# Fewer weight groups converted ahead of the second stage, the rest beside its first units, and three token blocks visited twice

## The chip, the core and the metric

One core of a Trainium2 chip runs the whole program. The metric is the device time of one execution in microseconds (us). The engines are PE (matrix products, with PEld for its weight loads), DVE (VectorE), ACT (ScalarE), POOL (GpSimd) and SP, whose queue issues every DMA of this kernel. Each engine works through its own list of instructions in order.

## What is computed

Causal attention with a decay for 8 batches of 8 heads (576 rows, 64 columns a head), and then a feed-forward network on the 4608 rows of 512 columns that it leaves:

```
scores = q @ k.T / sqrt(64) + cum[:, None] - cum[None, :]   # cum: running sum of log(clip(f, 1e-4, 1))
attn = softmax(causal(scores)) ; x = attn @ v               # x: 4608 x 512
h = x @ w_in                                                # 512 x 2048
g = h * erf(softplus(h))
out = g @ w_out                                             # 2048 x 512
```

All values are float32.

## The kernel before

The program has two stages on the same engines.

**Attention.** A loop over `t` runs 64 half-steps and 5 more to drain. A half-step is half of the query blocks of a pair of heads. It is a software pipeline: at `t` the kernel forms the scores of half-step `t` (PE, `scores`), reduces them with the decay (DVE, `reduce`, L459), takes exponentials of `t-1` (ACT), scales those of `t-2` (`normalize`: a small sum and reciprocal on DVE, L476 and L477, the scaling `pr` on POOL, L481), transposes those of `t-3` (PE, L493; 12 transposes in an even half-step and 13 in an odd one), multiplies `t-4` with the values (PE, L520), and stores `t-5` (`xo`, L529 to L533, to `xt_d` in memory, L535). The order of the instructions of PE, ACT, DVE and POOL is that of the source; SP's is set by the scheduler.

**Weight conversion.** Into the same loop the kernel puts the conversion of the weights. They come as 64-bit words and are turned into float32 by integer operations on DVE and then split into a rounded high part and a low part, so that a product is three fast ones. The weights fall into `NU` = 8 groups, each of four pieces (two of `w_out`, two of `w_in`). For a piece, `words` issues three DVE operations (L333 to L335) and `joined` two (L342, L351). Both pieces of `w_in` end in one tile `wa`, of which there is a single buffer. POOL then forms sums of its blocks (`combine`, L370), ACT rounds (`out_high` L357, `in_high` L374), POOL subtracts the rounded part (`out_low` L362, `in_low` L380), and SP stores high and low parts to `wo_d` and `wi_d` (L358, L363, L375, L382). A table `work` holds these in steps, a group starting every 8 steps; one step is done per half-step from t = 4, and two from t = 60.

**Second stage** (class `Moe`). Tokens are taken in `NV` = 6 blocks of 768, features in the 8 groups; a unit is one group for one block, 48 units in all. x is split for one level of Strassen's scheme: three differences of halves, a fourth later (`sub`, L119), and each of seven terms is rounded (ACT, L125) and its rest taken (POOL, L129). `up(u)` has seven products of six matmuls (L165) into four PSUM banks `pha`, `phb`, `phx`, `phy`; the first four products open the banks, and the last three accumulate into `pha`, `phx` and `phy`, after DVE has copied or added what stood there (L171, L175). `activate` has softplus and erf on ACT, `gate` multiplies on DVE (L204, tile `e`), `round_gate` splits the result into `gh` (ACT) and `gl` (POOL, L212). `down(u, tb)` has six matmuls for each of six token tiles (L223), with four PSUM buffers `y`; `flush` adds `y` to `ys` in SBUF (DVE, L232, L235), and after the eighth group stores it. `middle(u)` issues `down(u)` on PE, and meanwhile the activation and gates of `u+1` between the flushes, then `prepare(u)` with some steps of the next block's x. Behind it stands `up(u+2)`. The first two `up` stand in the draining half-steps 64 to 67. Weights are loaded per unit, `wi` (L145) and `wo` (L151), each with two buffers.

Of the kernel before, what the change touches and what calls it, by code (L numbers as in the profile page):

```python
# [21 lines left out]
P = 128  # L22
# [38 lines left out]
X0 = 32  # L61
TABLES = "natural_log_exp_and_others"
# [9 lines left out]
class Moe:  # L72
# [39 lines left out]
    def x_steps(self, v):  # L112

        nc, raw = self.nc, self.raw

        def sub(name, a, b, kd):
            if kd == 0 and name not in ("12",):
                raw[v, name] = self.half(name, v)
            nc.gpsimd.tensor_tensor(out=raw[v, name][:, kd], in0=raw[v, a][:, kd], in1=raw[v, b][:, kd], op=ALU.subtract)  # L119

        def high(n, nm):
            pool = self.xq if v % 2 and n > 2 else self.xp
            self.xs[v, n] = x = pool.tile([P, 2, 2, TB], F32R, name=f"xs{v}_{n}", tag="xs",
                                          bufs=10 if pool is self.xp else 4)
            nc.scalar.copy(out=x[:, 0], in_=raw[v, nm])  # L125

        def low(n, nm, kd):
            x = self.xs[v, n]
            nc.gpsimd.tensor_tensor(out=x[:, 1, kd], in0=raw[v, nm][:, kd], in1=x[:, 0, kd].bitcast(F32),  # L129
                                    op=ALU.subtract)  # L130
# [11 lines left out]
    def load_wi(self, u):  # L142
        if u < self.n:
            self.wi[u] = w = self.wp.tile([P, 2, 7, 2, P], F32R, name=f"wi{u}", tag="wi", bufs=2)
            self.nc.sync.dma_start(out=w.rearrange("p h i k f -> p (h i k f)").bitcast(F32),  # L145
                                   in_=self.wi_d[u % NU])

    def load_wo(self, u):
        if u < self.n:
            self.wo[u] = w = self.wop.tile([P, 2, 2, DM], F32R, name=f"wo{u}", tag="wo", bufs=2)  # L150
            self.nc.sync.dma_start(out=w.rearrange("p f h e -> p (f h e)").bitcast(F32),  # L151
                                   in_=self.wo_d[u % NU])
# [73 lines left out]

    def flush(self, u, tb, y):
        nc = self.nc
        v, a = divmod(u, NU)
        if a == 0:  # L230
            self.y[v, tb] = self.yp.tile([P, DM], F32, name=f"ys{v}_{tb}", tag="ys", bufs=8)
            nc.vector.tensor_copy(out=self.y[v, tb], in_=y)  # L232
            return
        ys = self.y[v, tb]
        nc.vector.tensor_tensor(out=ys, in0=y, in1=ys, op=ALU.add)  # L235
        if a == NU - 1:
            row = v * NW + tb * P
            nc.sync.dma_start(out=self.out[row:row + P], in_=ys)

    def prepare(self, u):  # L240

        v, a = divmod(u, NU)
        if v + 1 == NV:
            return
        if a == 0:
            self.load_x(v + 1)
            self.later = self.x_steps(v + 1)
        else:
            for _ in range(-(-len(self.later) // (NU - 1 - a)) if a < NU - 1 else 0):
                self.later.pop(0)()  # L250

    def middle(self, u):
# [17 lines left out]


@with_exitstack
def attention_moe(ctx, tc, q2, k2, vp, f, w_in, w_out, out):
# [28 lines left out]

    moe = Moe(tc, xt_d, out, xp, wp)
    moe.wi_d, moe.wo_d = wi_d, wo_d

    moe_pools = ctx.enter_context(ExitStack())
    with ExitStack() as ph:
        early = ExitStack()
        cv = ph.enter_context(tc.tile_pool(name="cv", bufs=2))
# [17 lines left out]

        def words(u):

            raw = raws[u]  # L330
            tops[u] = top = cv.tile([P, DM], F32, name=f"wtop{u}", tag="wtop", bufs=3)
            topi = top.bitcast(I32)
            nc.vector.tensor_scalar(out=topi, in0=raw[1], scalar1=0x7FFFFFFF, scalar2=None, op0=ALU.bitwise_and)  # L333
            nc.vector.tensor_scalar(out=top, in0=top, scalar1=TINY, scalar2=None, op0=ALU.max)
            nc.vector.tensor_scalar(out=topi, in0=topi, scalar1=3, scalar2=0x3FFFFFFF,  # L335
                                    op0=ALU.logical_shift_left, op1=ALU.bitwise_and)

        def joined(u):

            a, i = divmod(u, 4)  # L340
            raw, topi = raws.pop(u), tops[u].bitcast(I32)
            nc.vector.scalar_tensor_tensor(out=topi, in0=raw[0], scalar=29, in1=topi,  # L342
                                           op0=ALU.logical_shift_right, op1=ALU.bitwise_or)
            out_, top, sign = topi, topi, raw[1]
            if i > 1:
                if i == 2:
                    sums[a] = cv.tile([P, 8, 2 * P], F32, name=f"wa{a}", tag="wa", bufs=1)
                out_ = (sums[a][:, 4:6] if i == 3 else sums[a][:, ::7]).bitcast(I32)
                top, sign = (x.rearrange("p (i n) -> p i n", i=2) for x in (top, sign))
                del tops[u]  # L350
            nc.vector.scalar_tensor_tensor(out=out_, in0=sign, scalar=-0x40000000, in1=top,  # L351
                                           op0=ALU.bitwise_and, op1=ALU.bitwise_or)
            load_weight(u + 2)

        def out_high(a, i):
            highs[a, i] = hi = cv.tile([P, DM], F32R, name=f"wohi{a}_{i}", tag="wohi", bufs=1)
            nc.scalar.copy(out=hi, in_=tops[4 * a + i])  # L357
            nc.sync.dma_start(out=wo_d[a][:, 2 * i * DM:(2 * i + 1) * DM], in_=hi.bitcast(F32))  # L358

        def out_low(a, i):  # L360
            top, hi = tops.pop(4 * a + i), highs.pop((a, i))
            nc.gpsimd.tensor_tensor(out=top, in0=top, in1=hi.bitcast(F32), op=ALU.subtract)  # L362
            nc.sync.dma_start(out=wo_d[a][:, (2 * i + 1) * DM:(2 * i + 2) * DM], in_=top)  # L363

        def combine(a, *which):
            w = sums[a]
            for n in which:
                x, y, op = {3: (7, 5, ALU.add), 2: (0, 7, ALU.subtract), 1: (3, 0, ALU.subtract),
                            6: (4, 1, ALU.subtract)}[n]
                nc.gpsimd.tensor_tensor(out=w[:, n], in0=w[:, x], in1=w[:, y], op=op)  # L370

        def in_high(a, lo, hi):
            highs[a] = part = cv.tile([P, 4, 2 * P], F32R, name=f"whi{a}_{lo}", tag="whi", bufs=1)[:, :hi - lo]
            nc.scalar.copy(out=part, in_=sums[a][:, lo:hi])  # L374
            nc.sync.dma_start(out=wi_d[a][:, lo * 256:hi * 256], in_=part.rearrange("p i f -> p (i f)").bitcast(F32))  # L375

        def in_low(a, *which):
            for lo, hi in which:
                w = sums[a][:, lo:hi]
                nc.gpsimd.tensor_tensor(out=w, in0=w, in1=highs[a][:, lo % 4:lo % 4 + hi - lo].bitcast(F32), op=ALU.subtract)  # L380
                if hi == 7:
                    nc.sync.dma_start(out=wi_d[a][:, 7 * 256:], in_=sums.pop(a)[:, :7].rearrange("p i f -> p (i f)"))  # L382

        work = defaultdict(list)
        for a in range(NU):
# [3 lines left out]
            for i in range(2):  # L389
                work[8 * a + 2 * i + 2].append((out_high, a, i))  # L390
                work[8 * a + 2 * i + 3].append((out_low, a, i))
# [270 lines left out]
```

## Time and profile before

| | |
|---|---|
| runs, us | 1203.05, 1198.08, 1201.11; median 1201.11 |
| profiled execution, us | 1199.8 |
| its span, first to last instruction, us | 1198.0 |
| mean granted TensorE clock | 0.966 |
| attention loop | to about 454 us |
| first down product | 461.98 us |
| chain that ended last | PE 61% of the span |

A row of a group of instructions gives line, engine, operation, output<-input, shapes and count, then busy time in us and the mean of one in ns, then the idle time of the engine before them and who ended it. A row of waits gives who waited for whom, the total in us, how often, and the longest. A row of the timeline gives start and length in us. A row of a stretch gives its length, the busy time of PE, PEld, DVE, ACT and POOL with their counts, the granted clock, the DMA share and GB/s. A row of one tile's instructions gives the shortest, median and longest in ns.

### The profile page before, as it was taken

The numbers are of one execution on the slowest core, as the hardware profiler recorded it, in microseconds if no ns is written. First come the engines' busy times: TensorE is split into PE (matmuls) and PEld (weight loads), VectorE is DVE, ScalarE is ACT, GpSimd is POOL, SyncE is SP. The second block draws the span as 40 slices with busy tenths as digits, with TensorE's granted clock in tenths as the row PEclk, the third lists the DMA queues.
The fourth block names the chain that finished last, engine by engine and source line by source line (L and its number), as shares of the span: only waits on it lengthen the run. The fifth ranks groups of instructions, "written<-read, shape, count | busy, mean of one in ns | idle before, by whom it ended". The sixth has DMA issues, their size and how long they took to land.

```text
span 1198.0 us, 21626 instructions
## 1 busy us (share of the span) xinstructions
PE 1102.8 (92%) x7552; PEld 973.9 (81%) x7552; DVE 801.6 (67%) x1899; ACT 697.0 (58%) x1519; POOL 606.6 (51%) x732
## 2 busy tenths in 40 slices
PE   5997979788697686999999999999999999999998
PEld 3886767667586575999999999999999999999997
DVE  4997979789797843666666555556666666665555
ACT  3785758576575552565555655555565556555553
POOL 2466657676676651555345534554455435552223
PEclk9998989898898898999999999999999999999999
DMA  6697997878778535556655675567555754566532
GB/s 246 205 318 251 330 314 281 277 258 256 248 254 292 190 132 207 194 193 234 230 188 191 246 247 181 180 221 244 186 194 216 266 200 176 184 214 221 193 132 88
DMA packets 66124, 265.94 MB, mean 222 GB/s; under 512 B 7008, under 2 KB 13152, under 8 KB 53728
## 3 DMA queue, kind: packets, MB, share of 16 engines
q1 hardware_dynamic: 66016, 264.56, 63.1%
q8 instruction: 60, 0.98, 0.3%
q14 instruction: 48, 0.39, 0.1%
HBM read 222.45 MB, written 42.09 MB: 221 GB/s over the span
## 4 chain that ended last, share of the span: by engine, by line
PE 61%; DMA 1%; DVE 0%; issue 0%; SPq 0%
PE y L223 33%; PE pha L165 8%; PE phy L165 8%; PE phx L165 8%; PE phb L165 4%; DMA wo<-wo_d 1%; DVE ys L235 0%; SPq L535 0%; SPq L151 0%
## 5 line engine op out<-in xcount | busy, mean ns | idle before, releaser
L212 POOL TENSOR_TENSOR gl<-e,gh 128x384 fp32r<-128x384 f32 x192 | 221.9, 1188 | 415.9 <-PE y L223 215.0
L223 PE MATMUL y<-wo,gh 128*128 128x512 f32 x1152 | 357.5, 391 | 8.8 <-DMA wo<-wo_d 8.8
L223 PEld LDWEIGHTS y<-wo,gh 128*128 128x128 f32 x1152 | 216.7, 189 | 52.4 <-issue 9.0
L481 POOL TENSOR_SCALAR pr<-pr,st 128x576 f32<-128x576 f32 (+4 forms) x320 | 164.4, 537 | 159.3 <-DVE st L477 120.7
L235 DVE TENSOR_TENSOR ys<-y,ys 128x512 f32<-128x512 f32 x252 | 174.3, 692 | 99.4 <-PE y L223 99.4
L223 PE MATMUL y<-wo,gl 128*128 128x512 f32 x576 | 225.8, 392 | 0.0
L471 ACT ACTIVATE pr<-pr,st 128x576 f32<-128x576 f32 (+3 forms) x320 | 176.7, 556 | 43.4 <-DVE st L459 43.2
L520 PE MATMUL o<-pt,v 128*64 128x128 f32 (+1 forms) x1920 | 116.8, 280 | 68.8 <-DVE xo L533 40.3
L520 PEld LDWEIGHTS o<-pt,v 128*64 128x64 f32 x1920 | 107.4, 151 | 79.7 <-DVE xo L533 62.4
L459 DVE CUSTOM_DVE_ANT_0 pr<-s,c 128x576 f32<-128x576 f32 (+3 forms) x320 | 136.2, 485 | 21.1 <-PE s L441 19.3
L436 PE MATMUL s<-k,q 64*128 64x320 f32 (+4 forms) x768 | 128.7, 448 | 13.2 <-DMA k<-in_k_dram 8.5
L502 ACT COPY pt<-t 128x512 f32<-128x512 f32 x128 | 73.8, 578 | 107.2 <-PE t L493 107.2
L211 ACT CAST gh<-e 128x384 fp32r<-128x384 f32 x192 | 93.8, 513 | 65.7 <-DVE e L204 65.2
L194 ACT ACTIVATE e<-pha 128x384 f32<-128x384 f32 x48 | 23.6, 491 | 178.5 <-PE pha L165 178.5
L223 PEld LDWEIGHTS y<-wo,gl 128*128 128x128 f32 x576 | 108.6, 189 | 22.9
L436 PEld LDWEIGHTS s<-k,q 64*128 64x128 f32 x768 | 87.4, 208 | 45.5 <-issue 19.8
L171 DVE TENSOR_TENSOR u<-phx,u 128x384 f32<-128x384 f32 x96 | 53.5, 558 | 99.1 <-PE phx L165 99.0
L165 PE MATMUL pha<-xs,wi 128*128 128x384 f32 x576 | 116.9, 337 | 0.6 <-DVE st L459 0.6
L165 PE MATMUL phy<-xs,wi 128*128 128x384 f32 x576 | 115.3, 334 | 0.0
L165 PE MATMUL phx<-xs,wi 128*128 128x384 f32 x576 | 115.3, 334 | 0.0
L194 ACT ACTIVATE e<-u 128x384 f32<-128x384 f32 x144 | 74.7, 522 | 56.0 <-DVE u L171 56.0
L165 PEld LDWEIGHTS pha<-xs,wi 128*128 128x128 f32 x576 | 102.3, 188 | 4.6 <-PE o L520 0.7
(64 smaller groups left out, 1617.4 us busy)
## 6 DMA issues: line engine op xcount, KB each, us to landing
wi<-wi_d SPq DMA_DIRECT2D x48, 1792.0 KB, 7.3
wo<-wo_d SPq DMA_DIRECT2D x48, 1024.0 KB, 4.8
v<-in_vp_dram SPq DMA_DIRECT2D x32, 576.0 KB, 7.2
c<-cum_d SPq DMA_DIRECT2D x62, 288.0 KB, 5.4
q<-in_q_dram SPq DMA_DIRECT2D x32, 320.0 KB, 5.4
k<-in_k_dram SPq DMA_DIRECT2D x32, 288.0 KB, 5.0
xt_d<-xo SPq DMA_DIRECT2D x32, 288.0 KB, 7.2
r<-xt_d SPq DMA_DIRECT2D x24, 384.0 KB, 5.4
```

What stands on the lines that cost most here:

```text
L165: nc.tensor.matmul(out=ps, lhsT=wi[:, w, n, kd], rhs=xs[:, x, kd], start=not part and kd == 0 and i == 0, stop=kd == 1 and i == 2, skip_gr ...
L194: nc.scalar.activation(out=e_, in_=h[c], func=AF.Softplus)
L211: nc.scalar.copy(out=gh, in_=e_)
L212: nc.gpsimd.tensor_tensor(out=gl, in0=e_, in1=gh.bitcast(F32), op=ALU.subtract)
L223: nc.tensor.matmul(out=y, lhsT=x[:, cs], rhs=wo[:, i, w], start=i == 0 and n == 0, stop=i == 1 and n == 2)
L235: nc.vector.tensor_tensor(out=ys, in0=y, in1=ys, op=ALU.add)
L436: nc.tensor.matmul(out=s[j][:, at:at + k1 - k0], lhsT=q[h, PAD + START[i]:PAD + END[i]], rhs=k[h, k0:k1], start=i > 0, stop=k1 < END[i])
L459: nc.vector.tensor_tensor_reduce(out=to[:, ::-1] if j else to, in0=score, in1=decay_, scale=-0.125, scalar=BIG, op0=ALU.add, op1=ALU.min, ...
L471: nc.scalar.activation(out=seg, in_=seg, func=AF.Exp, bias=st[:, 0, j, m:m + 1], scale=-1.0, accum_out=st[:, 1, j, m:m + 1])
L481: nc.gpsimd.tensor_scalar(out=seg, in0=seg, scalar1=st[:, 2, j, m:m + 1], scalar2=1.0, op0=ALU.mult, op1=ALU.mult)
L502: nc.scalar.copy(out=pt[:, 512 * a:512 * a + 512], in_=b)
L520: nc.tensor.matmul(out=o[h, to:to + width], lhsT=v[:, ch, h], rhs=pt[:, at[j]:at[j] + width], start=n == 0, stop=n == len(parts) - 1, skip ...
```

## The change

- **Pace.** The loop of attention follows a new table: the steps of a group are spread (`joined` of the first piece of `w_in` moves from step 5 to 6 of its group, `in_low` from steps 11 and 13 to 10 and 12, `out_low` a step later), and `due` says how many steps are done by half-step `t`: two a half-step in t = 0 to 3, then 37 over the next 60, then one a half-step. Five groups are through by then, and the sixth and part of the seventh are under way.
- **Rest.** 19 steps are left for `middle`, which calls `convert` twice a unit: once among the flushes (after the fourth) and once after the gates.
- **Visits.** Blocks 0, 1 and 2 are first visited with groups 0 to 4, then with 5 to 7, and blocks 3 to 5 with all 8. Partial sums `ys` of the first visits go to memory (`part_d`) and are loaded again by `want_y`. The number of visits goes from 6 to 9, and x is loaded and split for each. The x of a visit is loaded two visits ahead.
- **Engine of the differences.** After the first visit's, `sub` runs on DVE instead of POOL.
- **Pools.** `cv` (tiles of conversion) stays for the whole program, so the pool of `wo` no longer takes its place, but that of the attention tiles `wk`; the x pool `xq` has 3 buffers instead of 4.
- **Small.** The sum in `normalize` adds a constant tile instead of a constant.

```diff
+NU1 = 5
+HALF = 3
...
+        first, second, every = (list(range(*r)) for r in ((NU1,), (NU1, NU), (NU,)))
+        self.visits = ([(v, first) for v in range(HALF)] + [(v, second) for v in range(HALF)]
+                       + [(v, every) for v in range(HALF, NV)])
...
+        engine = nc.vector if k else nc.gpsimd
...
-            nc.gpsimd.tensor_tensor(out=raw[v, name][:, kd], in0=raw[v, a][:, kd], in1=raw[v, b][:, kd], op=ALU.subtract)
+            engine.tensor_tensor(out=raw[k, name][:, kd], in0=raw[k, a][:, kd], in1=raw[k, b][:, kd], op=ALU.subtract)
...
+    def want_y(self, u):
...
+                if a:
+                    self.nc.sync.dma_start(out=ys, in_=self.part_d[self.visits[k][0] * NTB + tb])
...
-            nc.sync.dma_start(out=self.out[row:row + P], in_=ys)
+            nc.sync.dma_start(out=self.out[row:row + P] if a == NU - 1 else self.part_d[v * NTB + tb], in_=ys)
...
+        if i == n - 2:
+            self.load_x(k + 2)
...
-        order = [("f", 0), ("f", 1), ("g", 0), ("f", 2), ("g", 1), ("f", 3), ("g", 2), ("f", 4), ("g", 3), ("f", 5)]
+        order = [("f", 0), ("f", 1), ("g", 0), ("f", 2), ("g", 1), ("f", 3), ("c", 0), ("g", 2), ("f", 4), ("g", 3),
+                 ("f", 5)]
...
             for n in range(4):
                 self.round_gate(u + 1, n)
+            convert()
             self.prepare(u)
...
-            for i in range(4):
-                work[8 * a + 2 * i].append((words, 4 * a + i))
-                work[8 * a + 2 * i + 1].append((joined, 4 * a + i))
+            for u, steps in enumerate(((0, 1), (2, 3), (4, 6), (5, 7))):
+                work[8 * b + steps[0]].append((words, 4 * a + u))
+                work[8 * b + steps[1]].append((joined, 4 * a + u))
...
-            for _ in range(1 if t < NH - 4 else 2):
-                if t >= 4 and work:
-                    for call, *args in work.pop(0):
-                        call(*args)
+            due = 2 * t + 2 if t < 4 else 8 + (8 * NU1 - 3) * (t - 3) // (NH - 4) if t < NH else 8 * NU1 + 6 + t - NH
+            while 8 * NU + 5 - len(work) < due:
+                convert(work)
...
-            nc.vector.tensor_scalar(out=st[:, 1], in0=st[:, 1], scalar1=1e-9, scalar2=None, op0=ALU.add)
+            nc.vector.tensor_tensor(out=st[:, 1], in0=st[:, 1], in1=tiny[:, :2 * n].rearrange("p (j m) -> p j m", j=2),
+                                    op=ALU.add)
```

DVE in unit 0 of the second stage, before, from the fourth flush (`ys` <- `y`; `e` are gates, `u` the copy and adds of the next `up`):

```order
L232 COPY ys0_3_5726<-y0_3_5684 128x512
L204 TENSOR_TENSOR e1_22_5707<-e1_22_5707,u3_1_5547 128x384
L232 COPY ys0_4_5729<-y0_4_5691 128x512
L204 TENSOR_TENSOR e1_12_5711<-e1_12_5711,u2_1_5546 128x384
L232 COPY ys0_5_5732<-y0_5_5698 128x512
L175 COPY u2_2_5788<-pha2_5760 128x384
```

The same place after the change (`wtop` is a piece under conversion, `r` and `rT` are x and its differences):

```order
L253 COPY ys0_3_5585<-y0_3_5609 128x512
L351 TENSOR_SCALAR wtop25_5652<-wraw25_5494 128x512
L352 TENSOR_SCALAR wtop25_5652<-wtop25_5652 128x512
L353 TENSOR_SCALAR wtop25_5652<-wtop25_5652 128x512
L215 TENSOR_TENSOR e1_22_5632<-e1_22_5632,u3_1_5446 128x384
L253 COPY ys0_4_5586<-y0_4_5616 128x512
L215 TENSOR_TENSOR e1_12_5636<-e1_12_5636,u2_1_5445 128x384
L253 COPY ys0_5_5587<-y0_5_5623 128x512
L360 SCALAR_TENSOR_TENSOR wtop25_5652<-wraw25_5494,wtop25_5652 128x512
L369 SCALAR_TENSOR_TENSOR wtop25_5652<-wraw25_5494,wtop25_5652 128x512
L131 TENSOR_TENSOR rT1_1_5686<-r12_1_5576,r11_1_5574 128x384 x2
L131 TENSOR_TENSOR rT2_1_5689<-r22_1_5578,rT1_1_5686 128x384 x2
```

Five operations of conversion and six subtracts (two more follow these rows) now stand ahead of DVE's copy of `pha`.

SP at the end of attention, before (`[waits ...]` names the semaphores, DMAHW0 to 7 being the lanes of earlier DMAs, in turn):

```order
L375 DMA wi_d7_90<-whi7_4_5593 128x768 [waits DMAHW2_49,Activation_49]
L382 DMA wi_d7_90<-wa7_5229 128x1792 [waits DMAHW3_49,Pool_49]
L145 DMA wi3_5619<-wi_d3_86 128x3584 [waits DMAHW4_49,PE_49]
L535 DMA xt_d_82<-xo31_5621 128x576 [waits DMAHW5_49,DVE_49]
L151 DMA wo0_5659<-wo_d0_91 128x2048 [waits DMAHW3_49,DMAHW6_49,DMAHW2_49,DMAHW0_49]
```

The same place after:

```order
L156 DMA wi3_5516<-wi_d3_105 128x3584 [waits DMAHW3_49,PE_49]
L570 DMA xt_d_83<-xo31_5518 128x576 [waits DMAHW4_49,DVE_49]
L344 DMA wraw26_5553<-in_w_in_dram 128x1024 [waits DMAHW6_49,DMAHW5_49,DVE_49]
L400 DMA wi_d5_107<-wa5_5411 128x1024 [waits Pool_49]
L162 DMA wo0_5570<-wo_d0_110 128x2048 [waits DMAHW4_49,DMAHW7_49,DMAHW0_49,PE_49]
```

The first load of `wo` waited for lane 3, the store of the weights `wa`; now it waits for lane 4, the last store of x, and stands behind a store of weights that are still being converted.

SP in units 2 to 4 after the change (`r11_2` and `r12_2` are x of the third visit; before, the load of `wi6` stood among the other weight loads):

```order
L118 DMA r11_2_6187<-xt_d_83 128x2x384 [waits DMAHW7_49,Activation_49]
L118 DMA r12_2_6189<-xt_d_83 128x2x384 [waits DMAHW0_49,Activation_49,Pool_49]
L156 DMA wi6_6080<-wi_d1_103 128x3584 [waits DMAHW1_49,PE_49]
L162 DMA wo5_6195<-wo_d0_110 128x2048 [waits DMAHW2_49,PE_49]
L393 DMA wi_d6_108<-whi6_0_6170 128x1024 [waits DMAHW3_49,Activation_49]
```

The load of `wi6` has moved behind two x loads that wait for ACT and POOL.

More of the change, by code (lines that the diff above doesn't have):

```diff
@@ L269, in middle @@
         self.load_wo(u + 2)
+        self.want_y(u + 1)
 @with_exitstack
@@ L301, in attention_moe, with load_weight @@
     wp = ctx.enter_context(tc.tile_pool(name="wp", bufs=1))
+    cv = ctx.enter_context(tc.tile_pool(name="cv", bufs=2))
     moe = Moe(tc, xt_d, out, xp, wp)
-    moe.wi_d, moe.wo_d = wi_d, wo_d
+    moe.wi_d, moe.wo_d, moe.part_d = wi_d, wo_d, part_d
+    raws, tops, sums, highs = {}, {}, {}, {}
+    def load_weight(u):
+        a, i = divmod(u, 4)
+        if a == NU:
+            return
+        r = (2 * a + i) * P
+        raw = cv.tile([P, 2 * DM], I32, name=f"wraw{u}", tag="wraw")
+        raws[u] = [raw.rearrange("p (n w) -> p n w", w=2)[:, :, w] for w in range(2)]
+        nc.sync.dma_start(out=raw, in_=w_in[a, i - 2] if i > 1 else w_out[r:r + P])
@@ new lines, in joined @@
+    def joined(u):
+        a, i = divmod(u, 4)
+        raw, topi = raws.pop(u), tops[u].bitcast(I32)
+        nc.vector.scalar_tensor_tensor(out=topi, in0=raw[0], scalar=29, in1=topi,
+                                       op0=ALU.logical_shift_right, op1=ALU.bitwise_or)
+        out_, top, sign = topi, topi, raw[1]
+        if i > 1:
+            if i == 2:
+                sums[a] = cv.tile([P, 8, 2 * P], F32, name=f"wa{a}", tag="wa", bufs=1)
+            out_ = (sums[a][:, 4:6] if i == 3 else sums[a][:, ::7]).bitcast(I32)
+            top, sign = (x.rearrange("p (i n) -> p i n", i=2) for x in (top, sign))
+            del tops[u]
+        nc.vector.scalar_tensor_tensor(out=out_, in0=sign, scalar=-0x40000000, in1=top,
+                                       op0=ALU.bitwise_and, op1=ALU.bitwise_or)
+        load_weight(u + 2)
@@ new lines, in out_high, with out_low @@
+    def out_high(a, i):
+        highs[a, i] = hi = cv.tile([P, DM], F32R, name=f"wohi{a}_{i}", tag="wohi", bufs=1)
+        nc.scalar.copy(out=hi, in_=tops[4 * a + i])
+        nc.sync.dma_start(out=wo_d[a][:, 2 * i * DM:(2 * i + 1) * DM], in_=hi.bitcast(F32))
+    def out_low(a, i):
+        top, hi = tops.pop(4 * a + i), highs.pop((a, i))
+        nc.gpsimd.tensor_tensor(out=top, in0=top, in1=hi.bitcast(F32), op=ALU.subtract)
+        nc.sync.dma_start(out=wo_d[a][:, (2 * i + 1) * DM:(2 * i + 2) * DM], in_=top)
@@ new lines, in combine, with in_high @@
+    def combine(a, *which):
+        w = sums[a]
+        for n in which:
+            x, y, op = {3: (7, 5, ALU.add), 2: (0, 7, ALU.subtract), 1: (3, 0, ALU.subtract),
+                        6: (4, 1, ALU.subtract)}[n]
+            nc.gpsimd.tensor_tensor(out=w[:, n], in0=w[:, x], in1=w[:, y], op=op)
+    def in_high(a, lo, hi):
+        highs[a] = part = cv.tile([P, 4, 2 * P], F32R, name=f"whi{a}_{lo}", tag="whi", bufs=1)[:, :hi - lo]
+        nc.scalar.copy(out=part, in_=sums[a][:, lo:hi])
+        nc.sync.dma_start(out=wi_d[a][:, lo * 256:hi * 256], in_=part.rearrange("p i f -> p (i f)").bitcast(F32))
@@ L306, in attention_moe, with convert @@
+    def convert(work):
+        for call, *args in work.pop(0) if work else ():
+            call(*args)
     moe_pools = ctx.enter_context(ExitStack())
@@ L328, in words @@
[L328 to L385, printed above, removed]
-            for i in range(4):
-                work[8 * a + 2 * i].append((words, 4 * a + i))
-                work[8 * a + 2 * i + 1].append((joined, 4 * a + i))
-            for i in range(2):
-                work[8 * a + 2 * i + 2].append((out_high, a, i))
-                work[8 * a + 2 * i + 3].append((out_low, a, i))
-            for n, args in enumerate([(combine, a, 3, 2), (combine, a, 1, 6), (in_high, a, 0, 4), (in_low, a, (0, 2), (2, 4)),
-                                      (in_high, a, 4, 7), (in_low, a, (4, 6), (6, 7))]):
-                work[8 * a + 8 + n].insert(0, args)
@@ L395, in attention_moe @@
-        work = [work[n] for n in range(8 * NU + 6)]
         def log_clipped(x):
@@ L555, in attention_moe @@
         load_weight(1)
+        work = schedule(range(NU))
         for t in range(NH + 5):
@@ L613, in attention_moe @@
                 moe.ps_h = moe_pools.enter_context(tc.tile_pool(name="ps_h", bufs=1, space=PSUM, side="right"))
-        assert not work and not moe.later and not pts and not held and not vals
+        assert not moe.later and not pts and not held and not vals
     moe.wop = ctx.enter_context(tc.tile_pool(name="wop", bufs=1))
@@ L627, in attention_moe @@
             moe.load_wi(u + 4)
+    assert not work
 def kernel(q, k, v, f, moe_w_in, moe_w_out):
```

118 lines of the change are left out of this document (73 added, 45 removed).

## The prediction

> **What bounds the kernel now.** I read the page's busy table first, then the busy time by stretch, the waits of the attention loop, and its PE timeline.
>
> ```profile
> PE 1102.8 (92%) x7552; PEld 973.9 (81%) x7552; DVE 801.6 (67%) x1899; ACT 697.0 (58%) x1519; POOL 606.6 (51%) x732
> 64.00:117.00 53.00, 44.31 (x499) 37.55 (x497) 44.08 (x149) 35.80 (x108) 32.92 (x52) 0.92 0.84 287
> 473.00:1190.00 717.00, 717.00 (x3605) 649.81 (x3604) 432.27 (x739) 405.03 (x680) 322.27 (x296) 1.00 0.56 201
> ```
>
> The page's shares mix two regimes. In the second stage (473 to 1190 us; the columns are PE, PEld, DVE, ACT, POOL) PE has no gap at all: 717.0 of 717 us. In one period of the attention loop (64 to 117 us) PE and DVE both have 44 of 53 us, so both stand still for a sixth of it. The waits from 34 to 400 us tell why:
>
> ```profile
> DVE wa L351 <- DMA wi_d<-wa: 40.3, 6, 7.5
> DVE pr L459 <- PE s L441: 9.0, 9, 1.8
> ```
>
> DVE waits six times for the store of the rounded weight sums before `joined` may overwrite the single `wa` buffer, 40.3 us in all, and for PE only 9.0 us. So in this loop DVE ends last. What would PE do without it? A bank of 13 transposes marks every odd half-step:
>
> ```profile
> 34.48 1.73 PE L493 MATMUL t<-ident,pr 128*128 128x128 f32 x13
> 44.32 1.73 PE L493 MATMUL t<-ident,pr 128*128 128x128 f32 x13
> 94.52 1.74 PE L493 MATMUL t<-ident,pr 128*128 128x128 f32 x13
> 108.21 1.73 PE L493 MATMUL t<-ident,pr 128*128 128x128 f32 x13
> 400.15 1.73 PE L493 MATMUL t<-ident,pr 128*128 128x128 f32 x13
> ```
>
> The pair from 34.48 to 44.32 took 9.84 us with PE back to back; the pair from 94.52 took 13.69. From 34.48 to 400.15 lie 29 pairs: 365.7 us, against 29 x 9.84 = 285.4. That is 80.3 us above PE's own pace, half of it the DMA wait.
>
> **The attention loop.** These are the DVE operations of a conversion step, over the whole run:
>
> ```profile
> L333 DVE TENSOR_SCALAR wtop<-wraw 128x512 int32<-128x512 int32 x32 | 20.7, 647 | 0.0
> L334 DVE TENSOR_SCALAR wtop<-wtop 128x512 f32<-128x512 f32 x32 | 16.9, 529 | 1.1
> L335 DVE TENSOR_SCALAR wtop<-wtop 128x512 int32<-128x512 int32 x32 | 17.0, 533 | 1.1
> L342 DVE SCALAR_TENSOR_TENSOR wtop<-wraw,wtop 128x512 int32<-128x512 int32 x32 | 39.0, 1218 | 0.1
> L351 DVE SCALAR_TENSOR_TENSOR wtop<-wraw,wtop 128x512 int32<-128x512 int32 x16 | 20.0, 1248 | 0.6
> L351 DVE SCALAR_TENSOR_TENSOR wa<-wraw,wtop 128x512 int32<-128x512 int32 x16 | 11.1, 692 | 43.2 <-DMA wi_d<-wa 40.3 <-ACT pt L502 2.6
> ```
>
> Together 124.7 us in 64 steps, 1.95 each. In those 29 pairs (t = 4 to 61) there were 58 steps; by the new `due` there are 35. DVE was occupied for 365.7 - 40.3 - 9.0 = 316 us; less 23 x 1.95 = 45 it is 271, which fits under PE's 285. The `wa` wait goes because the last `in_low` of a group now stands at step 12 and the overwriting `joined` at step 14: two steps are about 3.2 half-steps, 16 us, against at most 7.5 us of waiting before. So the ceiling of the gain is 80.3. What is late next is DVE again, 95% full. Five pairs without a DMA wait (44.32 to 94.52) ran 50.2 us, 1.0 above pace, so 6 us is the low end of what remains; the 3.9 us of the pair after 94.52 (a cluster of port waits, below), once per each of five groups and added to it, is the high end, 25. I take 15, the middle: **-65**.
>
> The new start: 8 steps in t = 0 to 3, where DVE waits for PE, as here:
>
> ```profile
> 30.35 0.62 DVE L459 CUSTOM_DVE_ANT_0 pr<-s,c 128x448 f32<-128x448 f32 x1 [3.44 <-PE s L441]
> ```
>
> Three such gaps hold about 10 us, and 8 undisturbed steps (1.3 us each, by the shortest durations further down) are 10.6. Nothing to 4 us is lost; the third and fourth raw weights are loaded only after the first `joined`, so I take **+2.5**.
>
> The loop's last two half-steps, t = 62 to 64:
>
> ```profile
> 419.62 1.30 PE L165 MATMUL pha<-xs,wi 128*128 128x384 f32 x6 [0.63 <-DVE st L459]
> 423.89 1.72 PE L493 MATMUL t<-ident,pr 128*128 128x128 f32 x13
> ```
>
> 400.15 to 423.89 is 23.7 us; PE's own pace is 9.84 plus the four products from 419.62 to 423.89, 4.3. The gap of 9.6 is a DMA wait and two steps per half-step. I take **-9** (-6 to -11). The chain behind it, through the first activation, has its order kept. The replaced add in `normalize` is one small DVE operation for another: nothing.
>
> **The handover.** In the order of SP, the first `wo` load waited for the last store of weights; now it waits for the last store of x.
>
> ```profile
> 453.75 0.32 SPq L535 DMA_DIRECT2D xt_d<-xo  x1
> 454.25 0.86 SPq L151 DMA_DIRECT2D wo<-wo_d  x2
> xt_d<-xo SPq DMA_DIRECT2D x3, 288.0 KB, 2.1
> 461.98 10.79 PE y L223 x36
> ```
>
> That store lands in 2.1 us in this quiet stretch (420 to 480 us), so `wo` goes out 1.7 us later; 2 to 6 if a weight load runs beside it: **+3**. SP also has a store of the sixth group ahead of `wo`, whose POOL work should be done by then.
>
> **The second stage.** One unit, PE and DVE:
>
> ```profile
> 743.68 8.20 PE y L223 x36
> 755.91 1.20 PE L165 MATMUL pha<-xs,wi 128*128 128x384 f32 x6
> 756.95 1.20 PE L165 MATMUL phx<-xs,wi 128*128 128x384 f32 x6
> 751.92 0.69 DVE L235 TENSOR_TENSOR ys<-y,ys 128x512 f32<-128x512 f32 x1 [0.20 <-PE y L223]
> 752.99 0.56 DVE L175 COPY u<-pha 128x384 f32<-128x384 f32 x1 [0.37 <-PE pha L165]
> 755.07 0.56 DVE L171 TENSOR_TENSOR u<-phx,u 128x384 f32<-128x384 f32 x1 [0.48 <-PE phx L165]
> ```
>
> PE accumulates a second time into `pha` at 755.91 and into `phx` at 756.95, which need DVE's copy of the first and its add of the other. DVE is free at 752.61 and needs three times 0.56 for copy and two adds, so it may be late by 756.95 - 1.68 - 752.61 = 2.7 us. Two gaps of 0.20 between the flushes add 0.4 for work put among them: 3.1 us. A unit of conversion adds two steps, 2.6 us undisturbed: covered, barely. What breaks the cover is POOL:
>
> ```profile
> 62.40 1.81 DVE L342 SCALAR_TENSOR_TENSOR wtop<-wraw,wtop 128x512 int32<-128x512 int32 x1
> 62.39 1.28 POOL L362 TENSOR_TENSOR wtop<-wtop,wohi 128x512 f32<-128x512 f32 x1
> L119 POOL TENSOR_TENSOR rT<-r,rT 128x384 f32<-128x384 f32 x24 | 24.1, 1023 | 0.0
> L204 DVE TENSOR_TENSOR e<-e,u x144: 543/550/1227, 434.4 to 1185.4; 128x384 f32<-128x384 f32 x144
> ```
>
> ```profile
> L333 DVE TENSOR_SCALAR wtop<-wraw x32: 414/419/4954, 37.7 to 420.0; 128x512 int32<-128x512 int32 x32
> L334 DVE TENSOR_SCALAR wtop<-wtop x32: 426/428/841, 38.2 to 420.4; 128x512 f32<-128x512 f32 x32
> L335 DVE TENSOR_SCALAR wtop<-wtop x32: 426/427/1367, 38.6 to 420.9; 128x512 int32<-128x512 int32 x32
> L342 DVE SCALAR_TENSOR_TENSOR wtop<-wraw,wtop x32: 681/1198/1810, 42.5 to 421.4; 128x512 int32<-128x512 int32 x32
> L351 DVE SCALAR_TENSOR_TENSOR wtop<-wraw,wtop x16: 691/1104/1650, 43.3 to 405.5; 128x512 int32<-128x512 int32 x16
> ```
>
> L342 took 1.81 us at 62.40, when a POOL subtract had started just before it, and 0.68 at its shortest (the second block: shortest, median and longest in ns). Against their shortest the 160 DVE operations of conversion (124.7 us above) run 40 us over: w = 0.25 each. The moved x subtracts have no DVE row; POOL took 1.02 us (L119), and L204, a DVE operation of that shape, is 0.55 with a longest of 1.23. I take 0.56 + w.
>
> DVE steps of conversion lie in units 0 to 6, five operations each: 7 x (2.6 + 5w - 3.1). Units 0 and 5 also start a visit and get six subtracts: 12 x (0.56 + w). Units 10, 15, 18 and 21 get six alone, 24 and 32 five: 4 x (6(0.56 + w) - 2.7) + 2 x (5(0.56 + w) - 2.7). The sum is 6 + 81w. With w = 0.25, the row's value for the same operations: **+26**. The ends are w = 0, no wait (6), and w = 1.02, each operation behind one whole POOL subtract (89).
>
> The Trainium skill (SBUF — State Buffer, § SBUF: two separate sides) says that a GpSimd operation and a VectorE operation in a two-port mode or with two SBUF inputs exclude each other for the whole instruction, whichever starts first; rows 62.39 and 62.40 agree. By it an operation that falls behind a subtract each time gives w = 1.02 and the third rival below.
>
> After 9 us of idling PE took 10.79 us for the 36 products at 461.98, against 8.20 at 743.68. The Trainium skill (TensorE: Matmul & The Clock Gate, § What's actually happening) puts the clock at half after an idle window of about 3.4 us; the rows agree. If units 0 and 5 stall that long, 2.6 us each would come on top, inside the range.
>
> SP gets 18 stores and 18 loads of partial sums and three more loads of x; DMA has a share of 0.56 there, and a weight load (7.3 us) goes out 24 us before its first product, so they hide. One does not: the load for unit 6 now stands behind an x load that waits for the last rounding of unit 3. It goes out about 15 us late, which leaves 9: **+2** (0 to 4).
>
> ```profile
> wi<-wi_d SPq DMA_DIRECT2D x48, 1792.0 KB, 7.3
> ```
>
> **Sum.** -65 + 2.5 - 9 + 3 + 26 + 2 = -40.5 (-40.8 with the tenths). The profiled execution took 1199.8 us (span 1198.0), so 1159. The median of the three runs, 1201.1, is 1.3 above it, inside their spread of 5 us.
>
> **Rivals.**
> First, the cover holds: gates come before POOL's rounding in a unit, as L204's median of 0.55 says, so w is near 0 and the stage loses 6. 1199.8 - 66.8 + 6 = 1139; with 6 instead of 15 left in attention, 1130. Against it: POOL's four roundings run just where the steps are put.
> Second, attention gives back only the DMA waits: two engines at 95% and 100% in step with each other, POOL behind them, and 25 us of the 65 stay. 1159 + 25 = 1184. For it: every group had 3.9 us of excess without a DMA. Against: five pairs in a row at PE's pace with a step in each half-step.
> Third, slower: the port. At w = 1.02 the units lose 89 and the time is 1222. It turns the result at w = 0.75 (66.8 - 6 over 81) and makes it slower by over 0.5% at 0.83. For it: POOL is busier in these units than in attention, with roundings, weights and x lows. Against: 0.25 in attention, and waits that DVE wins are paid by POOL, which has time.
> That the change does nothing is excluded by the new order.
>
> **How the numbers follow.** About 0.5% is what a measurement of this kernel can tell from no change. My case (1145 to 1173) has 0.45, the first rival 0.23, the second 0.16, ports between (w of 0.4 to 0.75) 0.06, the third 0.10, of which 0.04 fall within 0.5% and 0.06 above. So faster 0.90, same 0.04, slower 0.06. The range for 8 in 10 runs from the first rival's low end to just past the second: 1128 to 1188.
>
> **What would show it.** No wait of DVE on the `wi_d` store; pairs near 9.9 us up to some 340 us; the first down product near 395; units 0 and 5 longest (19 us or more), units 1 to 6 near 16.5, all from 33 on 15.5. Wrong: a loop still at 12 us a pair, or units 0 to 6 over 22 us each.

## The result, and the profile after

The changed kernel takes 1207.35 us (median of five, 1206.06 to 1210.9) against 1198.97 for the kernel before in the same session: 1.0067 of it, 95% interval 1.0042 to 1.0093. It is slower by 0.7%; 1159 was forecast, with a range of 1128 to 1188. The profiled execution took 1209.55 us, span 1207.7.

The two halves of the forecast fared very differently. First the attention loop. These rows are the PE timeline (start, duration) and the busy time of the loop by engine (PE, PEld, DVE, ACT, POOL, then granted clock, DMA share, GB/s):

```profile
352.11 1.87 PE L528 MATMUL t<-ident,pr 128*128 128x128 f32 x13
396.22 1.19 PE L234 MATMUL y<-wo,gh 128*128 128x512 f32 x2 [13.63 <-DMA wo<-wo_d]
37.61:339.70 302.09, 293.05 (x3454) 246.34 (x3452) 267.07 (x961) 237.55 (x721) 217.24 (x359) 0.99 0.86 294
```

The marks of 13 transposes at 37.61, 339.70 and 352.11 stand where 34.48, 400.15 and 423.89 stood. The start costs 3.1 us, 29 pairs take 302.1 instead of 365.7 (-63.6), the next two half-steps 12.4 instead of 23.7 (-11.3), the way to the first down product 44.1 instead of 38.1 (+6.0). The down products begin at 396.2 instead of 462.0. The waits of DVE from 30 to 400 us (total, times, longest) have no store to `wi_d` among them any more, and PE is waited for longest:

```profile
DVE pr L493 <- PE s L475: 19.5, 22, 2.8
DVE wtop L351 <- DMA wo_d<-wtop: 3.6, 2, 2.5
```

So 65.8 us were won, and the second stage gave back more. From the first down product to the end of the span it took 736.0 us before and 811.4 now: +75.4. Its busy time in two stretches, and PE's waits from 390 us on:

```profile
396.22:845.00 448.78, 403.56 (x1881) 353.52 (x1882) 302.02 (x468) 232.67 (x381) 230.47 (x202) 0.95 0.64 225
845.00:1207.00 362.00, 356.84 (x1780) 320.87 (x1778) 227.36 (x384) 197.71 (x332) 136.88 (x120) 1.00 0.53 188
PE pha L176 <- DVE u L186: 40.3, 13, 7.3
PE phy L176 <- POOL xs L140: 4.7, 12, 1.1
PE phx L176 <- POOL xs L140: 1.1, 6, 0.2
PE pha L176 <- POOL xs L140: 1.0, 6, 0.2
```

PE, which had no gap there, is idle for 45 us of the first 449. Two releasers stand out: DVE's copy of `pha` (L186), thirteen times, and POOL's lows of x (L140), which are what the rounding leaves over of x. Units 0 and 5 are the longest, as forecast, but at 27.0 and 24.2 us, and units 1 to 3 take 20 and not 16.5. The table gives, for groups of units, the time above 15.5 us a unit, worked out from the start of each unit's first down product in the PE timeline, for this kernel and the main experiments below.

| units (what is special) | before | changed | subtracts on POOL | steps late | 21 to 8 split | one step a unit | tuned |
|---|---|---|---|---|---|---|---|
| 0 (first; steps and subtracts) | 2.4 | 11.4 | 4.1 | 2.1 | 11.9 | 7.8 | 2.9 |
| 1 to 4, 6 (conversion steps) | 0 | 17.6 | 16.8 | 20.7 | 17.9 | 2.2 | 0 |
| 5 (steps and subtracts) | 0 | 8.7 | 6.0 | 0.4 | 8.6 | 8.3 | 0 |
| 7 to 9, 11 to 14 | 0 | 0.7 | 3.7 | 4.0 | 0.6 | 15.8 | 7.7 |
| 10 (subtracts) | 0 | 4.4 | 0 | 0 | 2.9 | 7.3 | 1.2 |
| 15, 18, 21 (subtracts) | 0 | 18.4 | 0 | 0 | 18.9 | 20.1 | 0 |
| 16, 19, 22 (second of three) | 0 | 13.4 | 26.8 | 16.7 | 2.1 | 13.3 | 8.4 |
| 24, 32 (subtracts) | 0 | 3.2 | 0 | 0 | 3.2 | 3.2 | 0 |

### The profile page after: what moved, and what is told of

It reads as the page before. It is cut to its first block, busy times and chain, and to the rows that moved or that the text cites. A ratio compares the mean times of both kernels' runs of the same rounds, so it can differ in the third digit from the quotient of the medians.

```text
span 1207.7 us, 21855 instructions
## 1 busy us (share of the span) xinstructions
PE 1113.5 (92%) x7552; PEld 971.2 (80%) x7552; DVE 857.3 (71%) x1964; ACT 713.6 (59%) x1540; POOL 619.7 (51%) x734
## 5 line engine op out<-in xcount | busy, mean ns | idle before, releaser
L223 POOL TENSOR_TENSOR gl<-e,gh 128x384 fp32r<-128x384 f32 x192 | 234.5, 1250 | 454.5 <-PE y L234 370.3
L176 PE MATMUL pha<-xs,wi 128*128 128x384 f32 x576 | 125.3, 352 | 41.4 <-DVE u L186 40.3
L493 DVE CUSTOM_DVE_ANT_0 pr<-s,c 128x576 f32<-128x576 f32 (+3 forms) x320 | 136.4, 487 | 28.7 <-PE s L475 20.8
L176 PEld LDWEIGHTS pha<-xs,wi 128*128 128x128 f32 x576 | 105.3, 195 | 51.3 <-DVE u L186 41.7
L470 PE MATMUL s<-k,q 64*128 64x320 f32 (+4 forms) x768 | 121.1, 428 | 14.4 <-DMA k<-in_k_dram 8.3
L176 PE MATMUL phy<-xs,wi 128*128 128x384 f32 x576 | 123.5, 346 | 4.8 <-POOL xs L140 4.7
L176 PE MATMUL phx<-xs,wi 128*128 128x384 f32 x576 | 125.0, 352 | 1.1 <-POOL xs L140 1.1
L470 PEld LDWEIGHTS s<-k,q 64*128 64x128 f32 x768 | 80.9, 196 | 45.1 <-issue 20.4
L555 PE MATMUL o<-pt,v 128*64 128x128 f32 (+1 forms) x1920 | 104.4, 262 | 12.2 <-DVE xo L564 6.5
L555 PEld LDWEIGHTS o<-pt,v 128*64 128x64 f32 x1920 | 95.6, 139 | 22.1 <-issue 6.3
```

The costliest lines, as they stand in the source:

```text
L176: nc.tensor.matmul(out=ps, lhsT=wi[:, w, n, kd], rhs=xs[:, x, kd], start=not part and kd == 0 and i == 0, stop=kd == 1 and i == 2, skip_gr ...
L223: nc.gpsimd.tensor_tensor(out=gl, in0=e_, in1=gh.bitcast(F32), op=ALU.subtract)
L470: nc.tensor.matmul(out=s[j][:, at:at + k1 - k0], lhsT=q[h, PAD + START[i]:PAD + END[i]], rhs=k[h, k0:k1], start=i > 0, stop=k1 < END[i])
L493: nc.vector.tensor_tensor_reduce(out=to[:, ::-1] if j else to, in0=score, in1=decay_, scale=-0.125, scalar=BIG, op0=ALU.add, op1=ALU.min, ...
L555: nc.tensor.matmul(out=o[h, to:to + width], lhsT=v[:, ch, h], rhs=pt[:, at[j]:at[j] + width], start=n == 0, stop=n == len(parts) - 1, skip ...
```

## The experiments

**All groups in attention again** (run e1_all_attn). The order of the steps, the early start and the pace are left of the change, and with them its pools, its add in `normalize` and the loads of x two visits ahead.

```diff
-NU1 = 5
-HALF = 3
+NU1 = 8
+HALF = 0
...
-        engine = nc.vector if k else nc.gpsimd
+        engine = nc.gpsimd
...
```

> All eight groups are converted in attention again, by the changed kernel's order of steps and its pace (now 61 steps in 60 half-steps); every block is visited once; the x subtracts are on POOL as before. What is left of the change is the order of the steps, the early start and the pace. Theory A (the attention loop gains from both the vanished wait on the wi_d store and the lighter load): the wait is gone here too, DVE's own 316 us over 29 pairs sets the loop, 10.9 to 11.2 us a pair, so the first down product starts near 415 instead of 462, and with the second stage of before (736 us) the time is 1150 to 1160. Rival B (only the lighter load removes the wait; with one step in every half-step the store is waited for again): 1180 to 1200.

Measured: 1166.87 us, 0.9739 of before (0.9709 to 0.9769). Its loop and its first down product:

```profile
37.86:382.76 344.90, 313.67 (x3453) 262.00 (x3452) 315.73 (x1014) 244.86 (x729) 248.40 (x387) 0.98 0.85 292
434.85 1.19 PE L234 MATMUL y<-wo,gh 128*128 128x512 f32 x2 [10.79 <-DMA wo<-wo_d]
DVE wtop L351 <- DMA wo_d<-wtop: 9.2, 3, 5.6
```

The wait on the `wi_d` store is gone with eight groups too, so rival B falls; but a pair takes 11.9 us, not the 10.9 to 11.2 of theory A, the first down product starts at 434.9 and not near 415, and the time lies between the two ranges. DVE is busy for 315.7 of 344.9 us (before: 310.5 of 365.7), and in the waits from 38 to 340 us a store of `wtop` now stands where that of `wa` stood. What is left of the change gives 20.8 of the loop's 63.6 us, the three groups taken away 42.8. The second stage is that of before (735.3 us against 736.0). So the part of the change that moves three groups out of attention, with the second visits and the subtracts on DVE that come with it, is what makes the kernel slower: 1207 against 1167.

**The x subtracts back on POOL** (run e2_subs_pool), the last line of that diff alone.

> The changed kernel with the eight x subtracts of each visit back on POOL. Theory A (PE waits for DVE's copy of pha, which stands behind these subtracts in DVE's order): units 10, 15, 18, 21, 24 and 32 lose their excess (4.3 + 18.4 + 3.2 us), units 0 and 5 about 5 each, while units 16, 19 and 22, which wait for POOL's x lows, get 2 to 4 us longer each: 1175 to 1190. Rival B (DVE and POOL share one port, so the same work costs the same on either): units 0 to 24 no shorter, 1203 to 1210.

Measured: 1192.71 us in one run. By the table, units 10, 15, 18, 21, 24 and 32 lose all of their 26 us, unit 0 7.3 and unit 5 2.7; units 16, 19 and 22 become 4.5 us longer each, over the 2 to 4 expected, and the time is 2.7 us past theory A's range. Theory A holds for the subtracts. Rival B, equal cost on either engine, does not.

**The same work behind the copies** (run e3_late). Nothing is taken away; the steps and subtracts stand behind DVE's first four adds instead of ahead of the copy.

```diff
...
             moe.up(u + 2, 0)
+            convert(work)
+            convert(work)
+            if moe.units[u][1] != len(moe.visits[moe.units[u][0]][1]) - 2:
+                moe.prepare(u)
             moe.up(u + 2, 1)
```

> The changed kernel with both conversion steps of a unit, and the x steps except those of a visit's last unit but one, issued behind the first four up products and their DVE adds instead of ahead of them. No work is taken away. Theory A (what the second stage lost is DVE's place in the queue, and the slow clock behind each stall): units 1, 2, 4, 6, 10, 15, 18, 21, 24 and 32 fall to 15.5 to 16, unit 5 to under 17, unit 0 to 18 to 20; units 16, 19 and 22 keep their 4.4 us: 1150 to 1162. Rival B (DVE and POOL together have too much work there, or their port; the lateness moves to the activations and gates): half the 75 us or more stays, 1170 to 1200.

Measured: 1174.47 us, 0.979 (0.976 to 0.982). Where a unit has subtracts alone the whole excess goes (10, 15, 18, 21, 24, 32), and unit 5 too. Unit 10 of the changed kernel, DVE and then POOL:

```profile
598.35 1.83 DVE L131 TENSOR_TENSOR rT<-r,r 128x384 f32<-128x384 f32 x2
600.11 2.64 DVE L131 TENSOR_TENSOR rT<-r,rT 128x384 f32<-128x384 f32 x2
602.68 1.01 DVE L131 TENSOR_TENSOR r<-r,r 128x384 f32<-128x384 f32 x2
603.61 0.54 DVE L186 COPY u<-pha 128x384 f32<-128x384 f32 x1
595.75 5.30 POOL L223 TENSOR_TENSOR gl<-e,gh 128x384 fp32r<-128x384 f32 x4 [10.90 <-PE y L234]
601.02 1.32 POOL L140 TENSOR_TENSOR xs<-r,xs 128x384 fp32r<-128x384 f32 x1
```

and of this kernel:

```profile
585.61 0.56 DVE L186 COPY u<-pha 128x384 f32<-128x384 f32 x1 [0.37 <-PE pha L176]
589.21 1.02 DVE L131 TENSOR_TENSOR rT<-r,r 128x384 f32<-128x384 f32 x2
590.14 1.02 DVE L131 TENSOR_TENSOR rT<-r,rT 128x384 f32<-128x384 f32 x2
591.08 1.02 DVE L131 TENSOR_TENSOR r<-r,r 128x384 f32<-128x384 f32 x2
587.12 1.02 POOL L140 TENSOR_TENSOR xs<-r,xs 128x384 fp32r<-128x384 f32 x1
```

First, the copy goes ahead of the six subtracts and waits for PE (0.37 us), not PE for it. Second, the same six took 5.26 us (up to the start of the next operation) while POOL was at its roundings and a low (to 602.3), and 2.8 us once POOL had ended (588.1): how long DVE waits beside POOL is a matter of place. The Trainium skill (SBUF — State Buffer, § SBUF: two separate sides) has a VectorE operation with two SBUF inputs and a GpSimd operation that reads SBUF exclude each other for the whole instruction; the rows agree (subtracts of up to 1.37 us beside POOL, 0.55 without).

The rest of theory A missed. The time lies in rival B's range, and 41.5 of the 75.4 us stay (second stage 777.5 us): units 2 and 6 took 22 to 23 us. Ahead of their flushes two first halves of a conversion (`words`) follow each other, the second waits for a store out of `wtop`, and the flushes come late for PE. DVE's row in front of unit 2, and PE's waits from 410 to 845 us:

```profile
432.94 1.02 DVE L351 TENSOR_SCALAR wtop<-wraw 128x512 int32<-128x512 int32 x1 [2.45 <-DMA wo_d<-wtop]
PE y L234 <- DVE ys L255: 9.3, 3, 5.1
```

So for the conversion steps rival B is right in part: late, they miss another deadline.

**More x steps in the first unit of a three-unit visit** (run e4_split), 21 and 8 instead of 15 and 14.

> The changed kernel with the 29 x steps of a visit that stands behind a three-unit visit split 21 to 8 over its first two units instead of 15 to 14. Theory A (in units 16, 19 and 22 the up products wait for POOL's x lows because eight of them stand behind the gate's roundings in one unit, while POOL idles 8.7 us in the unit ahead): these three units fall from 20 to 15.5 to 16, units 15, 18 and 21 stay within 1 us: 1193 to 1196. Rival B (POOL's four more lows in units 15, 18 and 21 only shift the stall there): 1204 to 1209.

Measured: 1198.92 us in one run (span 1197.0). POOL and PE around unit 16 of the changed kernel, then of this one:

```profile
688.53 1.98 POOL L140 TENSOR_TENSOR xs<-r,xs 128x384 fp32r<-128x384 f32 x2
699.20 5.32 POOL L223 TENSOR_TENSOR gl<-e,gh 128x384 fp32r<-128x384 f32 x4 [8.69 <-PE y L234]
710.29 1.97 POOL L140 TENSOR_TENSOR xs<-r,xs 128x384 fp32r<-128x384 f32 x2
709.40 0.79 PE L176 MATMUL phx<-xs,wi 128*128 128x384 f32 x3 [0.17 <-POOL xs L140]
```

```profile
692.61 1.98 POOL L140 TENSOR_TENSOR xs<-r,xs 128x384 fp32r<-128x384 f32 x2
700.23 5.28 POOL L223 TENSOR_TENSOR gl<-e,gh 128x384 fp32r<-128x384 f32 x4 [5.64 <-PE y L234]
707.53 1.99 POOL L140 TENSOR_TENSOR xs<-r,xs 128x384 fp32r<-128x384 f32 x2
707.22 1.20 PE L176 MATMUL phx<-xs,wi 128*128 128x384 f32 x6
```

POOL idled 8.69 us and then worked to 712.3, while PE took each low as it came. With four more lows ahead of the pause, units 16, 19 and 22 lose 11.3 of their 13.4 us. The span is 10.7 us shorter, and the time stands between the two ranges, nearer theory A's: 0.7 us stays in each of the three units, and the start was 1.2 us later in this run.

**Both together** (run e5_both).

> The late steps (run e3_late) and the 21 to 8 split of x steps (run e4_split) together. In e3_late units 16, 19 and 22 still took 21.1 us each, with waits for POOL's x lows. Theory A: these fall to 15.5 to 16, 16 us in all, the rest as in e3_late: 1153 to 1159. Rival (with the DVE subtracts later, the lows are late whatever the split): 1163 to 1172.

Measured: 1169.69 us, 0.9749 (0.9728 to 0.9769): the rival's range, for another reason. Units 16, 19 and 22 fell only to 19.0 us, and PE waits for DVE there, 1.7 us each: by the order of the x steps two of the subtracts were left for that unit, where they stand ahead of the copy again.

**The clock** (run e6_warm). PE repeats products in the units where it stood idle; line numbers behind the diff's place are one higher here.

```diff
...
-            for kd in range(2):
+            for kd in [0, 1] * (1 + self.WARM.get(u - 2, 0) if n == 3 else 1):
```

> The changed kernel, in which PE repeats the six products of the fourth up product once to six times (1.04 us each) in the units where it stood idle for DVE's copy, so that PE is busy for most of the time it waited; the repeats overwrite the same bank. Nothing becomes ready earlier. Theory A (after an idle of 2 us or more PE runs at half clock, which made the next products 1.5 to 2.3 us long instead of 1.2): the slow products vanish, 15 to 20 us less in all, 1186 to 1193. Rival B (the long products wait for their operands one by one, or the clock does not look at idling): the time stays or rises by what the repeats overrun, 1204 to 1214.

Measured: 1197.51 us, 0.9983 (0.9969 to 0.9996), span 1192.5: shorter than the changed kernel, though PE does more. Behind the stall of unit 1, the changed kernel and then this one:

```profile
437.82 1.56 PE L176 MATMUL pha<-xs,wi 128*128 128x384 f32 x6 [2.11 <-DVE u L186]
439.19 2.25 PE L176 MATMUL phx<-xs,wi 128*128 128x384 f32 x6
```

```profile
433.86 1.34 PE L177 MATMUL pha<-xs,wi 128*128 128x384 f32 x6
435.19 1.32 PE L177 MATMUL phx<-xs,wi 128*128 128x384 f32 x6
```

The granted clock (third figure from the end) over the three slow microseconds of the changed kernel, and over the first stretch of this one, where the changed kernel had 403.56 of 448.78 us and 0.95:

```profile
438.80:441.80 3.00, 3.00 (x10) 2.73 (x10) 1.18 (x3) 0.90 (x2) 3.00 (x4) 0.50 0.02 5
393.57:840.00 446.43, 431.88 (x2112) 379.02 (x2113) 311.33 (x481) 238.96 (x390) 236.55 (x206) 1.00 0.66 233
```

So the long products are products at half the granted clock, and it does follow idling: rival B falls. From the first down product the end comes 12.5 us sooner (798.9 against 811.4), somewhat under theory A's 15 to 20, so the time stands between the two ranges. In units 24 and 32, whose stall was 1.03 us and was filled by one repeat (1.04), the 1.6 us stay, and the granted clock behind these stalls was 1.00 in the changed kernel too. So about 0.57 us behind such a stall is no clock at all, but PE following DVE's chain of adds (in unit 24 DVE's add out of `phx` ends at 857.80 and PE's next product into it starts at 857.86).

**One step a unit** (run e8_thin). The changed kernel's places, with one conversion step a unit in units 0 to 6 and two in units 7 to 12.

> The changed kernel with only the pace of conversion in the second stage changed: one step a unit in units 0 to 6 and two in units 7 to 12, where the changed kernel puts them. Theory A (a unit has 2 to 3 us of DVE slack ahead of PE's second product into pha; each step takes 2.5 to 3 us of it): units 1, 2, 4 and 6 lose their excess (13 us), units 7, 8, 9, 11 and 12 get 2 to 4.8 us each, unit 10 4 more: the time stays within 8 us of the changed kernel's, 1200 to 1216. Rival B (the first units are long for another reason than the conversion steps): units 1 to 6 keep over half of their excess.

Measured: 1211.14 us in one run. Units 1 to 4 and 6 keep 2.2 of 17.6 us, units 7 to 14 get 18 more: one step is covered and the second is not, as theory A has it. The sizes differ from it: units 7 and 8 take 6.4 and 6.8 us too long instead of 2 to 4.8, and units 11 and 12, which have none of DVE's conversion operations left, take 15.5.

**Spread and late** (run e7_spread). The late places, one step a unit at first, eight x steps in each of the first three units of a five-unit visit.

> As e5_both, with one conversion step a unit in units 0 to 6 and two in units 7 to 12 (19 as before), and eight x steps in each of the first three units of a five-unit visit. In e3_late units 1, 2, 3, 6 and 8 still took 1.2 to 7.4 us too long, by two steps in a row with a wait for a store into wtop's buffer between them. Theory A (with one step DVE's work fits where it is put): all units but 0 at 15.5 to 16.2, 1132 to 1143. Rival B (DVE and POOL block each other there, and a step in later units costs what it cost in the first ones): 1148 to 1160.

Measured: 1161.49 us, 0.9686 (0.966 to 0.9712), just past rival B's range. Units 1, 2, 4 and 6 are at 15.5 us, as theory A has it, but units 3 and 8, the last but one of a visit, kept 4.9 and 7.3 us, units 16, 19 and 22 3.5 each.

**Tuned by that profile** (run e10_tuned; the line numbers are those of the clock run).

```diff
+PACE = [1, 1, 1, 0, 2, 1, 2, 2, 0, 2, 2, 1, 2, 2]
...
+            share = {3: [23], 5: [8, 10, 10]}.get(n, [])
...
```

> As e7_spread, with the places tuned by its profile. There units 3 and 8 (last but one of a visit) were 4.9 and 7.3 us too long, units 16, 19 and 22 3.5 each, 9 and 11 together 3.6. Now units 3 and 8 get no conversion step and one x step left (8, 10, 10 and 1 in a five-unit visit), a three-unit visit takes 23 x steps in its first unit, so that all subtracts stand there, and units 4, 6, 12 and 13 take the steps. Theory A (each excess is one late operation in one engine's order): nearly all 26 us go, 1130 to 1142. Rival B (DVE and POOL have too much to do here together, so that the lateness moves on to other units): 1148 to 1162.

Measured: 1150.31 us, 0.9601 (0.9583 to 0.9619): the best of all, 4.0% under the kernel before and, by the ratios to it, 1.4% under the one with all groups in attention. Its time lies in rival B's range: only 8.6 of the 26 us went (from the first down product to the end 753.7 us, against 762.3 in run e7_spread). Its second stage, to 845 us:

```profile
396.00:845.00 449.00, 440.33 (x2165) 391.22 (x2164) 319.83 (x535) 262.97 (x437) 245.03 (x227) 0.99 0.70 251
PE y L235 <- DVE ys L256: 3.4, 2, 1.8
PE phx L177 <- POOL xs L141: 3.2, 6, 0.9
```

Some of the lateness did move on, to the flushes of units 8 and 11 and the lows of 16, 19 and 22; it went on shrinking, though. DVE and POOL do no less there than in the changed kernel (320 and 245 us against 302 and 230), with PE busy for 440 us of 449 instead of 404.

## Why the prediction was wrong, point by point

**The attention loop: right.** -65 was forecast, -63.6 measured, and the wait on the `wi_d` store is gone. DVE was put at 271 us and was busy for 267 (before, 310.5, where the working took 316). The remainder above PE's pace was put at 15 us and is 302.1 - 285.4 = 16.7; as 15 was only the middle between 6 and 25, that it came so near is in part luck. The start (+2.5) measured +3.1, the last two half-steps (-9) -11.3.

**The handover: at the edge of its bounds, mis-sized.** +3 was taken of "2 to 6", +6.0 measured. Loads and stores of weights now run beside the store of x, which lands after 5.7 us and not 2.1; the `wo` loads go out behind it. DMA issues from 380 to 400 us:

```profile
xt_d<-xo SPq DMA_DIRECT2D x1, 288.0 KB, 5.7
```

**The second stage: wrong.** +28 was forecast (26 for steps and subtracts, 2 for a load), +75.4 measured. It falls into three terms.

*DVE late for the copy*, the only one that was forecast: 40.3 us of idle PE against 26. The formula 6 + 81w was near enough, its w was not. It was taken as 0.25 "the row's value for the same operations", in attention. In the second stage the conversion's operations took, from 396 to 540 us:

```profile
L351 DVE TENSOR_SCALAR wtop<-wraw 128x512 int32<-128x512 int32 x7 | 3.9, 560 | 1.3 <-POOL gl L223 1.3
L352 DVE TENSOR_SCALAR wtop<-wtop 128x512 f32<-128x512 f32 x7 | 6.0, 860 | 0.2
L353 DVE TENSOR_SCALAR wtop<-wtop 128x512 int32<-128x512 int32 x7 | 6.4, 920 | 0.2
L360 DVE SCALAR_TENSOR_TENSOR wtop<-wraw,wtop 128x512 int32<-128x512 int32 x7 | 5.9, 842 | 0.0
L369 DVE SCALAR_TENSOR_TENSOR wa<-wraw,wtop 128x512 int32<-128x512 int32 x4 | 5.5, 1383 | 0.1
L369 DVE SCALAR_TENSOR_TENSOR wtop<-wraw,wtop 128x512 int32<-128x512 int32 x3 | 4.2, 1384 | 0.1
```

That is 31.9 us, against 18.5 for seven times the shortest (2.64): 13.4 over 35 operations, w = 0.38. For the subtracts, over the whole run:

```profile
L131 DVE TENSOR_TENSOR rT<-r,rT 128x384 f32<-128x384 f32 x32 | 31.7, 1022 | 0.0
L131 DVE TENSOR_TENSOR rT<-r,r 128x384 f32<-128x384 f32 x16 | 14.9, 972 | 0.0
L131 DVE TENSOR_TENSOR r<-r,r 128x384 f32<-128x384 f32 x16 | 13.1, 847 | 0.0
```

59.7 us over 64 is 0.93, 0.37 above 0.56. With 0.38 the formula gives 37, near the 40.3. (Its low end of 6 is 2.5 us too low: at w = 0 it lets units 1 to 4 and 6 gain 0.5 us each, which a covered unit cannot.) So the third rival's mechanism was at work, at somewhat over a third of its w. The prediction had the sentence that should have raised w ("POOL's four roundings run just where the steps are put") and used it only as an argument about a rival.

*The slow clock behind each stall*, left out of the sum: it was put at 2.6 us for each of two units, "inside the range". The granted clock falls to 0.50 behind nine of the thirteen stalls (units 0 to 3, 5, 10, 15, 18 and 21) and stays at 1.00 behind the four of 1.03 to 1.56 us. What is left of 75.4 after 40.3 and the 13.4 below is 21.7 us. If the 0.57 of the chain of adds holds behind all thirteen stalls, 7.4 of it is that chain and some 14 the clock; this split is an estimate. Summed over PE's busy time, the trace's granted clock makes the clock's share nearer 17 (19.2 us, against 2.5 in the kernel before). The repeats took 12.5 back. The Trainium skill (TensorE: Matmul & The Clock Gate, § What's actually happening), cited in the prediction, speaks of an idle window of about 3.4 us; here 2.11 us were enough, so the measurement decides, and the forecast drew the line too high. No line by length alone is right either: the same stall of unit 10, with the clock behind it, in the changed kernel and then in run e4_split:

```profile
604.21 1.31 PE L176 MATMUL pha<-xs,wi 128*128 128x384 f32 x6 [2.31 <-DVE u L186]
606.00:609.00 3.00, 3.00 (x11) 3.00 (x11) 0.70 (x2) 1.16 (x3) 0.00 (x0) 0.50 0.00 0
605.99 1.34 PE L176 MATMUL pha<-xs,wi 128*128 128x384 f32 x6 [2.31 <-DVE u L186]
607.80:610.80 3.00, 3.00 (x17) 2.78 (x16) 1.24 (x3) 1.60 (x4) 0.00 (x0) 1.00 0.20 38
```

That is why the table has 4.4 and 2.9 us for unit 10, where the two kernels do the same. What decides in such a case, no run here shows.

*POOL's x lows in units 16, 19 and 22*, not forecast at all: 13.4 us. The prediction counted the subtracts that the change sets into DVE's order and not the rest of the x steps: in a three-unit visit all 29 must fit into two units, where six units had shared them before. The split (run e4_split) took 11.3 of it away.

*The load for unit 6* (+2): no wait of PE for a `wi` load is in the trace; nothing.

**The rivals.** None was right as told. The first (cover holds) and the second (attention gives back less) did not happen. The third ended on the right side, but by its price alone: at the measured w of 0.38 it gives a gain of 30 us, and what turned it into a loss were the slow clock with the chain of adds and POOL's lows, which no rival had.

## What to carry to other kernels

An engine that looks two thirds busy still has a place for added work only where nobody waits for the operation behind it: read, for each added instruction, what stands next in that engine's order and who waits for it, and move the work behind that. When a stage is saturated on PE, count a stall as idle time plus the slow products that can follow it. And when a loop is cut into shorter visits, recount everything that was spread over its length, on every engine, not only what the edit names.

## What was not expected of the hardware

In the changed kernel stalls of 1.0 to 1.6 us left the granted clock at 1.00, one of 2.1 us made the next but one product 2.25 instead of 1.32 us long, one of 2.31 us lowered the clock in one run and not in another, and PE doing useless products through the stalls made the kernel faster than leaving it idle (0.9983 of before, 0.9969 to 0.9996, against 1.0067, 1.0042 to 1.0093). DVE beside POOL did not lose a whole POOL operation (1.02 us) each time: 0.37 to 0.38 us for an operation on average, from none, where POOL was idle, to 0.69 for L369 (1.38 against 0.69).
